# The gates of the second token group in another order on VectorE and ScalarE, and one last store in one piece

## The chip, the cores and the metric

The kernel runs on one core of one Trainium2 chip. The metric is the device time of one execution in microseconds; the number that is compared is the median over runs. Engines are named as in the profile: PE is TensorE (matmuls), PEld its weight loads, DVE is VectorE, ACT is ScalarE, POOL is GpSimd and SP is SyncE, which only issues DMAs here.

## What is computed

Three layers follow each other: an attention with global and local keys (2 x 8 heads, 768 positions, 64 wide), a first MoE block with a softmax and a layer norm, and a second block, `moe2`. The change lies in the second block alone:

```python
def _moe2_ref(x, w_in, w_out):          # x 1536 x 512, w_in 512 x 2048, w_out 2048 x 512
    h = x @ w_in
    g = h * (1.0 / (1.0 + np.exp(-h)))
    return (g @ w_out).astype(np.float32)
```

The gate is computed as (tanh(h / 2) + 1) * h, and the factor 0.5 is put on the output.

## The kernel before

The 1536 tokens are two groups of 768. Every float32 operand of a matmul is kept as two parts, a high one (`gh`, a copy in the matmul's reduced format, made by ScalarE) and a low one (`gl`, the difference, made by VectorE), and each product is three matmuls: high x high, high x low and low x high. Attention, the first block and the first group's second block are put in order by a list written out by hand (`ORDER`) and by loops behind it. All instructions of one engine run in the order in which the program text issues them.

The second group's up projection `h = x @ w_in` is done in `seven(i, fill, hook)`, L744, for eight steps `i`, each with 256 columns of `w_in`. A step forms its four blocks of h (two halves of the columns, two halves `s` of the tokens) from seven products P1 to P7, of six matmuls each, instead of eight. On TensorE a step runs

- P1 and P6 (`two`, L748), then a fill,
- P2 and P7, a fill,
- P5 and P4, a fill,
- P3, a fill.

A fill is `down` (L603): nine matmuls of the down projection with one gated block of the step before, so that TensorE has work while VectorE and ScalarE empty the products. In step 0 the fills are the last six matmuls of each of group 1's three output blocks, and `done` (L617) then copies that block out and stores it; for the third block this is an ACTIVATE of 128x1024 at L641 and a store issued on ScalarE's queue, from the buffer `sraw`.

PSUM has four tiles: three hold the output of `down`, so there is one for the products, and the next pair of products waits until the last one has been read. P1 is copied by ScalarE (L756) into `a`; VectorE adds up the rest (L746): `u = p6 + a`, then `a = p2 + a` and `b = p7 + u`, then `c = p5 + b`, `u = p5 + u`, `b = b - p4`, then `u = p3 + u`. The four tiles a, c, b, u are then the four blocks of h, and each goes through `gate` (L735): tanh on ScalarE into a buffer `e2` (two of them, L738), the gate on VectorE (L739), the high copy on ScalarE (L740); the low part (L733) is put on the list `later` and made by VectorE at the next call of `lows()`. Before the change the order in a step is: lows, gate a after P2 and P7, lows and gate c after P5 and P4, lows and gate b after P3, the last fill, gate u.

`hook` holds the weight sums for the next step (steps 1 to 6; in step 0 the splits of inputs `xprep`, in step 7 nothing): `wraw` (L694, VectorE, writes `sraw`) behind P1 and P6, `wsum` behind P2 and P7 (four adds of VectorE, L701 to L704, and the high copy L705 of 128x1024 on ScalarE), `wlow` (L709, VectorE) behind P3. P3, P5, P6 and P7 use these sums.

At the end `done` stores the three output blocks of group 2, 512 KB each: block 0 is copied by ScalarE (L641), block 1 by VectorE (L639), block 2 in halves, one by ScalarE (L633) and one by VectorE (L630), with a store for each half (L634 on ScalarE's queue, L631 on SP's).

Of the kernel before, what the change touches and what calls it, by code (L numbers as in the profile page):

```python
# [8 lines left out]
F32 = mybir.dt.float32  # L9
# [4 lines left out]
ACTF = mybir.ActivationFunctionType  # L14
ALU = mybir.AluOpType
# [41 lines left out]
def kernel(ctx, tc, q, k, v, n_global, n_local, w_in, w_out, g_ln, w2_in, w2_out, out):  # L57
    nc = tc.nc
    B, H, S, D = 2, 8, 768, 64
    NT, DM = out.shape  # L60
# [31 lines left out]
    ea = ExitStack()  # L92
# [12 lines left out]
    def f(ap):  # L105
        return ap.bitcast(F32)

    def psum():
        return ps.tile([128, 2, 512], F32, tag="p", name="p")
# [400 lines left out]
    for half in range(2):  # L510
        for kk in range(KD):
            c = slice(half * 512, half * 512 + 512)
            unit(wiw[kk * 128:(kk + 1) * 128, c, :], 0, lambda kk=kk, c=c: (wih[:, kk, c], wil[:, kk, c]))
    for half in range(2):
        for kk in range(0, KF, 2):
            c = slice(half * 256, half * 256 + 256)
            src = wow[kk * 128:(kk + 2) * 128, c, :].rearrange("(k p) n t -> p k n t", p=128)
# [16 lines left out]
    for i in range(NP):  # L534
        for j in range(2):
            c = slice(2 * j, 2 * j + 2)
            src = w2iw[j * 256:(j + 1) * 256, i * 256:(i + 1) * 256, :].rearrange("(k p) n t -> p k n t", p=128)
# [49 lines left out]
    def up(g, m, nbg=0):  # L587
        up_mm(g, m)
        up_act(g, m)
        up_mul(g, m)  # L590
        for s in range(2):
            e, hi, lo = gs[g, m, s]
            hilo(e, hi, lo)
            gs[g, m, s] = hi, lo
        bg(nbg)
# [3 lines left out]
    def words4(dt):  # L599
        x = cv.tile([128, 512, 2], I32, tag="cx", name="cx", bufs=CX)  # L600
        return x.rearrange("p n t -> p (n t)").bitcast(dt)
# [15 lines left out]
    def done(g, t3):  # L617
        o = acc[g][t3]
        rows = out.rearrange("(g s t p) d -> g t p s d", g=NG, s=2, p=128)[g, t3]
        if g == 0 and t3 == 1:  # L620
            for h in range(2):
                y = x2b[h][h].rearrange("p k n -> p (k n)")[:, 0:DM]
                nc.scalar.activation(out=y, in_=o[:, h], func=ACTF.Copy, scale=0.5)
                nc.sync.dma_start(out=rows[:, h], in_=y)
            return
        if g == 1 and t3 == 2:
            for h in range(2):
                y = words4(F32)[:, 0:DM]
                if h:
                    nc.vector.tensor_scalar(out=y, in0=o[:, h], scalar1=0.5, scalar2=None, op0=ALU.mult)  # L630
                    nc.sync.dma_start(out=rows[:, h], in_=y)  # L631
                else:
                    nc.scalar.activation(out=y, in_=o[:, h], func=ACTF.Copy, scale=0.5)  # L633
                    nc.scalar.dma_start(out=rows[:, h], in_=y)  # L634
            return
        y = sraw if g == 0 else words4(F32)
        y = y.rearrange("p (s n) -> p s n", s=2)
        if g and t3 == 1:
            nc.vector.tensor_scalar(out=y, in0=o, scalar1=0.5, scalar2=None, op0=ALU.mult)  # L639
        else:  # L640
            nc.scalar.activation(out=y, in_=o, func=ACTF.Copy, scale=0.5)  # L641
        (nc.sync if t3 == 1 else nc.scalar).dma_start(out=rows, in_=y)
# [74 lines left out]
    def product(i, n, p):  # L717
        src, k0, c, r = PROD[n]
        wh, wl = (w2h[i], w2l[i]) if src == "A" else sw[i]
        xh, xl = xop[r]  # L720
        c = slice(c * 128, (c + 1) * 128)
        j = 0
        for x, w in ((xh, wh), (xl, wh), (xh, wl)):
            for k in range(2):
                nc.tensor.matmul(p[:, 0:HG], lhsT=w[:, k0 + k, c], rhs=x[:, k, :], start=(j == 0), stop=(j == 5))  # L725
                j += 1

    later = []

    def lows():  # L730
        while later:
            e, hi, lo = later.pop(0)
            nc.vector.tensor_tensor(out=lo, in0=e, in1=f(hi), op=ALU.subtract)  # L733

    def gate(m, s, src):  # L735
        e = wk.tile([128, HG], F32, tag="e2", name="e2", bufs=2)
        hi, lo = (wk.tile([128, HG], F32R, tag=x, name=x, bufs=4) for x in ("gh", "gl"))
        nc.scalar.activation(out=e, in_=src, func=ACTF.Tanh, scale=0.5)  # L738
        nc.vector.scalar_tensor_tensor(out=e, in0=e, scalar=1.0, in1=src, op0=ALU.add, op1=ALU.mult)  # L739
        nc.scalar.activation(out=hi, in_=e, func=ACTF.Copy)  # L740
        later.append((e, hi, lo))
        gs[1, m, s] = hi, lo

    def seven(i, fill, hook):  # L744
        def add(dst, x, y, op=ALU.add):
            nc.vector.tensor_tensor(out=dst, in0=x, in1=y, op=op)  # L746

        def two(x, y):  # L748
            p = psum()
            for n, o in ((x, p[:, 0]), (y, p[:, 1])):  # L750
                product(i, n, o)
            return p[:, 0, 0:HG], p[:, 1, 0:HG]

        a, u, b, c = (cv.tile([128, 512], F32, tag="cc", name="cc", bufs=4)[:, 0:HG] for _ in range(4))
        p1, p6 = two("P1", "P6")
        nc.scalar.activation(out=a, in_=p1, func=ACTF.Copy)  # L756
        add(u, p6, a)
        lows()
        hook[0]()
        fill[0]()  # L760
        p2, p7 = two("P2", "P7")
        add(a, p2, a)
        add(b, p7, u)
        hook[1]()
        gate(2 * i, 0, a)
        fill[1]()
        p5, p4 = two("P5", "P4")
        add(c, p5, b)
        add(u, p5, u)
        add(b, b, p4, ALU.subtract)  # L770
        lows()
        gate(2 * i + 1, 1, c)
        fill[2]()
        p3 = psum()[:, 0]
        product(i, "P3", p3)
        add(u, p3[:, 0:HG], u)
        lows()
        hook[2]()
        gate(2 * i + 1, 0, b)
        fill[3]()  # L780
        gate(2 * i, 1, u)

    def guard():
        V = nc.vector
# [53 lines left out]
    with tc.manual_schedule():  # L838
        masks()
        for x in toks:  # L840
            nm, t = x.split(":")
            if nm == "CA":
                ea1.close()
                w2a = eb.enter_context(tc.tile_pool(name="w2a", bufs=1, side="right"))
                for i in range(2):
                    w2alloc(w2a, i)
            elif nm == "WK":
                ea.close()
                wk = eb.enter_context(tc.tile_pool(name="wk", bufs=1, side="right"))
                x2h = wk.tile([128, KD, G], F32R, name="x2h")  # L850
                x2l = wk.tile([128, KD, G], F32R, name="x2l")
            else:
                OPS[nm](int(t))
        fast = nc.values_load(flag, min_val=0, max_val=1)
        e1.close()
        w2b = eb.enter_context(tc.tile_pool(name="w2b", bufs=1, side="left"))
        for i in range(2, NP):
            w2alloc(w2b, i)
        bg(2)

        def fills(i):
            return [lambda z=z: down(1, *z) for z in ((2 * i, 0), (2 * i + 1, 1), (2 * i + 1, 0), (2 * i, 1))]

        def none():
            pass

        for z in range(2):
            down(0, 0, z)
        for m in range(2, KF2):
            if m < KF2 - 1:  # L870
                up(0, m, 2)
            else:
                up_mm(0, m)
                xprep(4)
                up_act(0, m)
                up_mul(0, m)
                xprep(9)
                up_hi(0, m)
                up_lo(0, m)
                xprep(5)  # L880
            for z in range(2):
                down(0, m - 1, z)
            if 10 <= m < 14:
                xprep(m - 10)
            if m == 13:
                sraw = words4(F32)
                sparts = [[words4(F32R) for _ in range(2)] for _ in range(2)]
            if 13 <= m < 15:
                wraw(m - 13)
                wsum(m - 13)  # L890
                wlow(m - 13)
        fill = [lambda t3=t3: [down(0, KF2 - 1, z, [t3]) for z in range(2)] for t3 in range(3)] + [none]
        for i in range(NP):
            if i == 0:
                hook = [lambda: [xprep(n) for n in (6, 7)], lambda: xprep(8), none]
            elif i < NP - 1:
                hook = [lambda: wraw(i + 1), lambda: wsum(i + 1), lambda: wlow(i + 1)]
            else:
                hook = [none] * 3
            seven(i, fill, hook)  # L900
            fill = fills(i)
        lows()
        for z in fill:
            z()
    eb.close()
# [2 lines left out]
    with tc.If(fast == 0):  # L908
# [12 lines left out]
        with tc.tile_pool(name="ga", bufs=1, side="left") as ga:  # L921
# [17 lines left out]
            with tc.For_i(0, B, 1) as bi, tc.For_i(0, H, 1) as hi:  # L939
                t3 = ga.tile([128, TB, D], F32, name="gv")  # L940
# [9 lines left out]
                for qb in range(TB):  # L950
# [31 lines left out]
                    o = psum()[:, 0, 0:D]  # L982
# [6 lines left out]
        with tc.tile_pool(name="gm", bufs=1, side="left") as gm:  # L989
# [8 lines left out]
            for src, dst, kk, c in full:  # L998
                units.append((src[kk * 128:(kk + 1) * 128, c * 512:(c + 1) * 512, :], 0, None, None))
                i = len(units) - 1  # L1000
# [7 lines left out]
            with tc.For_i(0, NTILE, 1) as ti:  # L1008
# [9 lines left out]
                e = gm.tile([128, FF], F32, name="ge")  # L1018
                u = gm.tile([128, FF], F32, name="gu")
# [78 lines left out]
```

## Time and profile before

| what | us |
|---|---|
| median of 3 runs (508.32 to 509.53) | 508.57 |
| the profiled execution, its own time | 509.89 |
| its span, from the first to the last instruction | 508.1 |
| TensorE busy in the span | 481.9 |
| VectorE busy | 378.3 |
| ScalarE busy | 268.4 |

The profile is of one execution, and all durations below are its. The busy share of an engine is an average over stages with different limits; the stage of the change is the last quarter of the span, from 365 us on, and it is read from the timeline: when each instruction started, how long it took, and what ended the idle time ahead of it. A matmul's start is to be relied on more than its end, which is modelled.

### The profile page before, as it was taken

The page shows a single profiled execution, that of the slowest core. Times are in us where ns is not written, and L with a number is a line of the kernel's source. Part 1 is how long each engine was busy: PE and PEld are TensorE (multiplying, and loading weights), DVE is VectorE, ACT ScalarE, POOL GpSimd, SP SyncE. Part 2 cuts the span into 40 slices and gives each one's busy share as a digit, 9 for nine tenths or more (in the row PEclk, how much of TensorE's full clock was granted, in tenths as well). Part 3 has the DMA queues.
Part 4 walks back from the last instruction along what each step waited for, and adds up shares of the span by engine and source line. Part 5 has one row for each costly group of instructions (what it writes and reads, how often), then busy time and mean ns, then how long its engine had stood idle before and what let it go on. Part 6 is the DMA issues. An engine that isn't in the chain of part 4 may idle for free.

```text
span 508.1 us, 8172 instructions
## 1 busy us (share of the span) xinstructions
PE 481.9 (95%) x2980; PEld 425.3 (84%) x2980; DVE 378.3 (74%) x847; ACT 268.4 (53%) x595; POOL 113.1 (22%) x149
## 2 busy tenths in 40 slices
PE   2789999999999999999999999999998999999993
PEld 2467789889888898999999999998887988889882
DVE  6999899866486577763698989998866676767651
ACT  5888997775566656443354545543562234232331
POOL 3664631221212233410233333332000000000000
PEclk9899999999999999999999999999998999999998
DMA  7964452332023021200324343300030000000003
GB/s 230 308 174 139 125 160 91 104 106 84 1 84 105 9 75 38 89 2 0 125 84 131 119 148 102 124 2 0 1 124 0 2 0 1 0 1 0 2 1 130
DMA packets 26115, 38.35 MB, mean 75 GB/s; under 512 B 1484, under 2 KB 13780, under 8 KB 26068
## 3 DMA queue, kind: packets, MB, share of 16 engines
q1 hardware_dynamic: 24580, 35.66, 21.9%
q10 hardware_dynamic: 1488, 2.10, 1.1%
q8 instruction: 25, 0.41, 0.3%
q14 instruction: 22, 0.18, 0.1%
HBM read 34.61 MB, written 3.15 MB: 74 GB/s over the span
## 4 chain that ended last, share of the span: by engine, by line
PE 89%; DVE 4%; DMA 2%; ACT 2%; issue 1%; SPq 1%; ACTq 0%; DVEq 0%
PE p L612 25%; PE p L499 14%; PE p L559 13%; PE p L415 12%; PE p L725 11%; PE p L357 4%; PE p L376 4%; PE p L310 3%; PE p L479 2%; DMA g<-in_moe_g_ln_dram 2%; DVE cc L147 1%; DVE A L329 1%; DMA cx<-in_moe_w_out_dram 1%; DVE cc L145 0%; ACT cx L641 0%
## 5 line engine op out<-in xcount | busy, mean ns | idle before, releaser
L612 PE MATMUL p<-w3h,gl 128*128 128x512 f32 x192 | 75.6, 394 | 0.0
L612 PE MATMUL p<-w3l,gh 128*128 128x512 f32 x192 | 75.5, 393 | 0.0
L612 PE MATMUL p<-w3h,gh 128*128 128x512 f32 x192 | 75.1, 391 | 0.0
L149 DVE SCALAR_TENSOR_TENSOR cc<-cx,cc 128x512 uint32<-128x512 uint32 x48 | 58.6, 1224 | 0.1
L415 PE MATMUL p<-wih,xT 128*128 128x512 f32 x192 | 50.5, 405 | 0.9 <-DVE negmax L329 0.9
L335 ACT ACTIVATE A<-A,negmax 128x256 f32<-128x256 f32 (+1 forms) x96 | 46.0, 481 | 8.6 <-DVE negmax L329 7.9
L329 DVE CUSTOM_DVE_ANT_0 A<-p,bias 128x256 f32<-128x256 f32 (+1 forms) x96 | 35.1, 395 | 15.4 <-PE p L357 10.3
L612 PEld LDWEIGHTS p<-w3h,gl 128*128 128x128 f32 x192 | 36.1, 188 | 7.8
L612 PEld LDWEIGHTS p<-w3l,gh 128*128 128x128 f32 x192 | 36.2, 188 | 6.4
L612 PEld LDWEIGHTS p<-w3h,gh 128*128 128x128 f32 x192 | 36.2, 189 | 6.2
L415 PEld LDWEIGHTS p<-wih,xT 128*128 128x128 f32 x192 | 34.4, 189 | 8.3 <-DVE negmax L329 1.1
L746 DVE TENSOR_TENSOR cc<-p,cc 128x384 f32<-128x384 f32 x48 | 25.2, 553 | 20.7 <-PE p L725 11.9
L170 POOL TENSOR_TENSOR w3l<-cc,w3h 128x512 fp32r<-128x512 f32 x16 | 23.4, 1462 | 60.4 <-ACT w3h L130 49.2
L740 ACT ACTIVATE gh<-e 128x384 fp32r<-128x384 f32 x32 | 16.8, 526 | 37.0 <-DVE e L739 36.4
L147 DVE SCALAR_TENSOR_TENSOR cc<-cx,cc 128x512 uint32<-128x512 uint32 x48 | 35.3, 738 | 0.1
L132 POOL TENSOR_SCALAR A<-A,sm 128x256 f32<-128x256 f32 (+1 forms) x34 | 20.3, 606 | 63.2 <-DVE sm L340 41.8
L705 ACT ACTIVATE cx<-cx 128x1024 fp32r<-128x1024 f32 x8 | 8.5, 1061 | 45.1 <-DVE cx L704 45.1
L739 DVE SCALAR_TENSOR_TENSOR e<-e,cc 128x384 f32<-128x384 f32 x32 | 17.7, 554 | 19.2 <-ACT e L738 19.2
L574 DVE SCALAR_TENSOR_TENSOR e<-e,p 128x384 f32<-128x384 f32 x32 | 16.3, 549 | 20.9 <-ACT e L568 20.9
L310 PE MATMUL p<-rk,rq 64*128 64x256 f32 (+1 forms) x192 | 26.9, 418 | 2.3 <-DMA rq<-in_q_dram 1.4
L568 ACT ACTIVATE e<-p 128x384 f32<-128x384 f32 x32 | 13.9, 487 | 27.3 <-PE p L559 27.3
L559 PE MATMUL p<-x2h,w2h 128*128 128x384 f32 x128 | 27.7, 338 | 0.0
(166 smaller groups left out, 1109.7 us busy)
## 6 DMA issues: line engine op xcount, KB each, us to landing
cx<-in_moe_w_in_dram SPq DMA_DIRECT2D x24, 512.0 KB, 3.7
cx<-in_moe_w_out_dram SPq DMA_DIRECT2D x24, 512.0 KB, 3.4
rq<-in_q_dram SPq DMA_DIRECT2D x12, 256.0 KB, 6.3
vf<-in_v_dram SPq DMA_DIRECT2D x12, 256.0 KB, 4.4
rk<-in_k_dram SPq DMA_DIRECT2D x11, 256.0 KB, 4.2
out_dram<-cx ACTq DMA_DIRECT2D x3, 512.0 KB, 3.3
out_dram<-x2b SPq DMA_DIRECT2D x2, 256.0 KB
out_dram<-cx SPq DMA_DIRECT2D x1, 512.0 KB, 4.2
```

The source lines that it names most:

```text
L147: V.scalar_tensor_tensor(out=y, in0=x[:, :, 0].bitcast(U32), scalar=29, in1=y, op0=ALU.logical_shift_right, op1=ALU.bitwise_or)
L149: V.scalar_tensor_tensor(out=y, in0=x[:, :, 1].bitcast(U32), scalar=0x80000000, in1=y, op0=ALU.bitwise_and, op1=ALU.bitwise_or)
L170: eng.tensor_tensor(out=lo, in0=w, in1=f(hi), op=ALU.subtract)
L310: nc.tensor.matmul(p[:, a, j, 0:128 * len(ks)], lhsT=rq[z, t % 3, pr, :], rhs=rk[z, W, pr, :], start=True, stop=True)
L329: nc.vector.tensor_tensor_reduce(out=x[:, c, 0:n], in0=p[:, a, j, 0:n], in1=bb, scale=-0.125, scalar=1e30, op0=ALU.add, op1=ALU.min, accum ...
L335: nc.scalar.activation(out=x[:, c, 0:n], in_=x[:, c, 0:n], func=ACTF.Exp, bias=negmax[:, t * H + h:t * H + h + 1], scale=-1.0, accum_out=s ...
L415: nc.tensor.matmul(p[:, half, :], lhsT=x[:, a, kk, :], rhs=w[:, kk, n], start=(i == 0), stop=(i == 11))
L499: nc.tensor.matmul(p[:, d], lhsT=x[:, kk, c], rhs=y[:, kk, sl], start=(i == 0), stop=(i == 3 * KF - 1))
L559: nc.tensor.matmul(p, lhsT=w[m // 2][:, kk, c], rhs=x[:, kk, s * HG:(s + 1) * HG], start=(i == 0), stop=(i == 11))
L612: nc.tensor.matmul(o, lhsT=x[:, c], rhs=w[m // 2][:, m % 2, :], start=(n == 0 and i == 0), stop=(n == KF2 - 1 and i == 2))
L725: nc.tensor.matmul(p[:, 0:HG], lhsT=w[:, k0 + k, c], rhs=x[:, k, :], start=(j == 0), stop=(j == 5))
L746: nc.vector.tensor_tensor(out=dst, in0=x, in1=y, op=op)
```

## The change

Group 2's gate is taken apart into `tanh`, `gated`, `high` and `low`, which issue one instruction each. In a step the order becomes: after P1 and P6 the copy of P1 and the add for P6, then high u of the step before (`rest`), low b of the step before, the hook, low u of the step before; after P2 and P7 the two adds, tanh a, the hook, gate a, high a; after P5 and P4 the three adds, tanh c, low a, gate c, tanh b, high c; the third fill; after P3 its add, gate b, low c, tanh u, high b, the hook, gate u. The instructions are the same as before. Behind the last step the high copy and the two lows that are left are issued. Block 2 of group 2 has no branch of its own in `done` any more: it is copied whole by ScalarE (L641) and stored by one store on ScalarE's queue.

```diff
--- before.py
+++ after.py
@@ -623,16 +623,6 @@
                 nc.scalar.activation(out=y, in_=o[:, h], func=ACTF.Copy, scale=0.5)
                 nc.sync.dma_start(out=rows[:, h], in_=y)
             return
-        if g == 1 and t3 == 2:
-            for h in range(2):
-                y = words4(F32)[:, 0:DM]
-                if h:
-                    nc.vector.tensor_scalar(out=y, in0=o[:, h], scalar1=0.5, scalar2=None, op0=ALU.mult)
-                    nc.sync.dma_start(out=rows[:, h], in_=y)
-                else:
-                    nc.scalar.activation(out=y, in_=o[:, h], func=ACTF.Copy, scale=0.5)
-                    nc.scalar.dma_start(out=rows[:, h], in_=y)
-            return
         y = sraw if g == 0 else words4(F32)
         y = y.rearrange("p (s n) -> p s n", s=2)
         if g and t3 == 1:
@@ -727,19 +717,25 @@
 
     later = []
 
-    def lows():
-        while later:
-            e, hi, lo = later.pop(0)
-            nc.vector.tensor_tensor(out=lo, in0=e, in1=f(hi), op=ALU.subtract)
-
-    def gate(m, s, src):
+    def low():
+        e, hi, lo = later.pop(0)
+        nc.vector.tensor_tensor(out=lo, in0=e, in1=f(hi), op=ALU.subtract)
+
+    def tanh(src):
         e = wk.tile([128, HG], F32, tag="e2", name="e2", bufs=2)
+        nc.scalar.activation(out=e, in_=src, func=ACTF.Tanh, scale=0.5)
+        return e
+
+    def gated(e, src):
+        nc.vector.scalar_tensor_tensor(out=e, in0=e, scalar=1.0, in1=src, op0=ALU.add, op1=ALU.mult)
+
+    def high(m, s, e):
         hi, lo = (wk.tile([128, HG], F32R, tag=x, name=x, bufs=4) for x in ("gh", "gl"))
-        nc.scalar.activation(out=e, in_=src, func=ACTF.Tanh, scale=0.5)
-        nc.vector.scalar_tensor_tensor(out=e, in0=e, scalar=1.0, in1=src, op0=ALU.add, op1=ALU.mult)
         nc.scalar.activation(out=hi, in_=e, func=ACTF.Copy)
         later.append((e, hi, lo))
         gs[1, m, s] = hi, lo
+
+    rest = []
 
     def seven(i, fill, hook):
         def add(dst, x, y, op=ALU.add):
@@ -755,30 +751,42 @@
         p1, p6 = two("P1", "P6")
         nc.scalar.activation(out=a, in_=p1, func=ACTF.Copy)
         add(u, p6, a)
-        lows()
+        if rest:
+            high(*rest.pop())
+            low()
         hook[0]()
+        if i:
+            low()
         fill[0]()
         p2, p7 = two("P2", "P7")
         add(a, p2, a)
         add(b, p7, u)
+        ea = tanh(a)
         hook[1]()
-        gate(2 * i, 0, a)
+        gated(ea, a)
+        high(2 * i, 0, ea)
         fill[1]()
         p5, p4 = two("P5", "P4")
         add(c, p5, b)
         add(u, p5, u)
         add(b, b, p4, ALU.subtract)
-        lows()
-        gate(2 * i + 1, 1, c)
+        ec = tanh(c)
+        low()
+        gated(ec, c)
+        eb_ = tanh(b)
+        high(2 * i + 1, 1, ec)
         fill[2]()
         p3 = psum()[:, 0]
         product(i, "P3", p3)
         add(u, p3[:, 0:HG], u)
-        lows()
+        gated(eb_, b)
+        low()
+        eu = tanh(u)
+        high(2 * i + 1, 0, eb_)
         hook[2]()
-        gate(2 * i + 1, 0, b)
+        gated(eu, u)
+        rest.append((2 * i, 1, eu))
         fill[3]()
-        gate(2 * i, 1, u)
 
     def guard():
         V = nc.vector
@@ -899,7 +907,9 @@
                 hook = [none] * 3
             seven(i, fill, hook)
             fill = fills(i)
-        lows()
+        high(*rest.pop())
+        low()
+        low()
         for z in fill:
             z()
     eb.close()
```

## Rows read from the trace of the kernel before

**Rows 1.** Page, part 1: busy us (share of span) x instructions

```profile
PE 481.9 (95%) x2980; PEld 425.3 (84%) x2980; DVE 378.3 (74%) x847; ACT 268.4 (53%) x595; POOL 113.1 (22%) x149
```

**Rows 2.** Timeline, PE, steps 1, 2, 7: start us, us, engine, line, operation, tiles

```profile
376.63 0.87 PE L725 MATMUL p<-x2a,w2h 128*128 128x384 f32 x4
...
396.26 0.86 PE L725 MATMUL p<-x2a,w2h 128*128 128x384 f32 x4
...
476.12 0.86 PE L725 MATMUL p<-x2a,w2h 128*128 128x384 f32 x4
...
489.71 0.39 PE L612 MATMUL p<-w3h,gh 128*128 128x512 f32 x1
```

**Rows 3.** Chain that ended last: start us, us, what; a fill in step 6

```profile
474.20 2.08 PE p L612 x9
```

**Rows 4.** Windows: us, PE, PEld, DVE, ACT, POOL busy; PEclk, DMA share, GB/s

```profile
381.00:381.50 0.50, 0.00 (x0) 0.00 (x0) 0.48 (x1) 0.00 (x0) 0.00 (x0) 1.00 0.00 0
...
384.00:384.50 0.50, 0.50 (x3) 0.50 (x2) 0.50 (x1) 0.00 (x0) 0.00 (x0) 0.50 0.00 0
```

**Rows 5.** Timeline, end of step 0 to P2 of step 1

```profile
377.32 1.01 ACT L641 ACTIVATE cx<-p 128x1024 f32<-128x1024 f32 x1
378.37 0.38 ACTq L642 DMA_DIRECT2D out_dram<-cx  x1
378.79 0.53 ACT L738 ACTIVATE e<-cc 128x384 f32<-128x384 f32 x1 [0.46 <-ACT cx L641]
...
379.95 0.53 ACT L740 ACTIVATE gh<-e 128x384 fp32r<-128x384 f32 x1 [0.63 <-DVE e L739]
380.38 0.51 ACT L738 ACTIVATE e<-cc 128x384 f32<-128x384 f32 x1
380.58 0.40 PE L612 MATMUL p<-w3h,gl 128*128 128x512 f32 x1
...
381.94 0.47 ACT L756 ACTIVATE cc<-p 128x384 f32<-128x384 f32 x1
382.45 0.56 DVE L746 TENSOR_TENSOR cc<-p,cc 128x384 f32<-128x384 f32 x1 [0.97 <-ACT cc L756]
383.06 1.08 PE L725 MATMUL p<-x2h,w2h 128*128 128x384 f32 x4 [2.08 <-DVE cc L746]
```

**Rows 6.** Timeline of step 2

```profile
397.31 1.20 PE L725 MATMUL p<-x2h,cx 128*128 128x384 f32 x6
...
405.48 1.06 ACT L705 ACTIVATE cx<-cx 128x1024 fp32r<-128x1024 f32 x1 [5.85 <-DVE cx L704]
...
406.98 0.56 DVE L739 SCALAR_TENSOR_TENSOR e<-e,cc 128x384 f32<-128x384 f32 x1 [1.54 <-ACT e L738]
407.46 1.01 DVE L746 TENSOR_TENSOR cc<-p,cc 128x384 f32<-128x384 f32 x2
408.39 0.55 DVE L746 TENSOR_TENSOR cc<-cc,p 128x384 f32<-128x384 f32 x1
408.99 1.31 PE L725 MATMUL p<-x2a,cx 128*128 128x384 f32 x6
...
411.28 1.22 DVE L709 TENSOR_TENSOR cx<-cx 128x1024 fp32r<-128x1024 f32 x1
```

**Rows 7.** Timeline of step 7: the adds for P5, then P3

```profile
486.78 1.02 DVE L746 TENSOR_TENSOR cc<-p,cc 128x384 f32<-128x384 f32 x2 [2.44 <-PE p L725]
...
488.66 1.21 PE L725 MATMUL p<-x2a,cx 128*128 128x384 f32 x6
```

**Rows 8.** Timeline, the last output block

```profile
500.33 0.60 ACT L633 ACTIVATE cx<-p 128x512 f32<-128x512 f32 x1 [0.51 <-PEq L908]
500.96 0.69 DVE L630 TENSOR_SCALAR cx<-p 128x512 f32<-128x512 f32 x1 [0.27 <-ACT cx L633]
501.68 0.40 SPq L631 DMA_DIRECT2D out_dram<-cx  x1
```

**Rows 9.** Windows at the end, columns as in rows 4

```profile
504.00:504.50 0.50, 0.00 (x0) 0.00 (x0) 0.00 (x0) 0.00 (x0) 0.00 (x0) 0.50 1.04 397
```

## The prediction, made before the changed kernel was run

> **What bounds the kernel now.** I read the page's busy table first: TensorE is busy for 95% of the span [rows 1], so only an order that lets TensorE run with fewer pauses or at a faster clock can pay. The change lies in the last stage, the eight steps of `seven`, so I went on to TensorE's timeline there. The reader should compare the starts of P1, the first product of a step. Step 1 begins at 376.63 and step 2 at 396.26, which is 19.63 us; from step 2 to step 7 there are five steps in 79.86 us, 15.97 each [rows 2]. Step 7, the last, has no weight sums to do beside its matmuls. From its P1 to the first matmul of its last fill it takes 13.59 us [rows 2], and a fill of nine matmuls takes 2.08 [rows 3]. So a step without a pause is 15.67 us. Against that, step 1 loses 3.96 us and steps 2 to 6 lose 0.30 each, 1.50 together: 5.46 us are there to be had in this stage, and no more.
>
> Where they go: in step 1 TensorE's last fill matmul starts at 380.58 and P2 only at 383.06, released by VectorE's L746 [rows 5]. The fill's pitch is 2.08 / 9 = 0.23, so P2 could have started at 380.81: a wait of 2.25 us. Behind it the granted clock is 0.50, the 1.2 GHz level, where it was 1.00 during the wait [rows 4]; the slow matmuls make up the rest of the 3.96, 1.71 us. In steps 2 to 6 the pause is ahead of P3: it starts 408.99 - 396.26 = 12.73 us into step 2, and 488.66 - 476.12 = 12.54 into step 7 [rows 2, 6, 7]; the other 0.1 is P3's own slow start (1.31 for six matmuls against 1.21).
>
> **The change part by part.** *Step 1's wait.* There is one PSUM tile for the products, so P2 waits until VectorE's `u = p6 + a` has read P6, and that waits for ScalarE's copy of P1 (L756). ScalarE runs its queue in order. Before, the queue between the large output copy L641 of group 1 and L756 holds tanh b, high b, tanh u, high u, and between these it waits twice for VectorE's L739: 378.79 to 381.94 [rows 5]. Afterwards tanh b stands ahead of L641, and high u (the `rest`) behind the copy. What is left between is tanh u and high b. Neither should wait there: high c ends ahead of L641 (377.32), and the low c that frees tanh u's buffer follows on VectorE behind at most one gate and one low of 0.56 us each (an L739 of [rows 6] for both), so by 378.6; high b's input is done in the same stretch. So, from rows 5: tanh u 378.79 (still behind the store's issue on ScalarE's queue at 378.37), high b one pitch later (380.38 - 379.95 = 0.43), the copy another 0.43 later at 379.65, the add 382.45 - 381.94 = 0.51 later, P2 383.06 - 382.45 = 0.61 later: 380.77. TensorE is ready at 380.81. The wait is gone with 0.04 us to spare, and with it the slow clock. Gain 3.96, or 3.7 if some tenths remain; I take 3.9.
>
> L641 itself must not move: it stood behind high c before and does so still. Tanh b, new ahead of high c, has to wait for the low of gate a (two `e` buffers); VectorE does that low just ahead of gate c, whose end high c needs anyway, so it has a pitch of 0.47 (407.46 - 406.98, [rows 6]) on VectorE to run in and costs 0 to 0.1.
>
> *Steps 2 to 6.* Before, tanh a stands behind the 1.06 us copy of the weight sums L705, so gate a (L739) starts at 406.98 and the first add that empties P5 only at 407.46, 11.20 us into the step [rows 6]. In step 7 without L705 the add starts at 10.66 [rows 7]. Afterwards tanh a is ahead of the sums, gate a runs right behind the sums' last add, which L705 waited for and which had ended at 405.46 (405.48 less a handover of 0.02), and is over at 406.0; VectorE is free when P4 ends, as in step 7. The third add ends about 0.5 us earlier, ahead of P3. Gain 5 x 0.30 = 1.50; between 0 (another wait is next) and 1.50 I take 1.5, since step 7's rows are the same matmuls in the same order. High a still stands behind L705: it is needed only by the next step's first fill.
>
> *What is moved on VectorE.* No gate instruction is added or removed. The wait of VectorE that is new is at the start of step 1: the weight sum L694 writes the buffer that group 1's last store (378.37) reads, and the adds for P2 and P7 are now close behind it. It is asked for near 381.1; by 381.00 no DMA moves a byte [rows 4], so it waits 0 to 0.5 us, and the adds are wanted only when P7 ends, two microseconds later. Cost nothing. The other is the low weight half L709: gate b now stands ahead of it (+0.47), but it is wanted by the last two matmuls of the next step's P6. P6 starts 397.31 - 396.26 = 1.05 into a step, four matmuls of 1.05 / 6 later they start, at 1.75. L709 started at 15.02 into step 2 and took 1.22; afterwards 15.2 to 16.4, against 15.67 + 1.75 = 17.42. One microsecond of cover.
>
> SP's queue loses one store and POOL has no work in this stage.
>
> *The last store.* Group 2's third output block is no longer copied in halves. Before: ScalarE's half at 500.33, VectorE's at 500.96, that is, behind the end of the first (its idle time is put down to L633), the last store issued at 501.68 [rows 8]. Afterwards one copy of 128x1024, 1.01 us (L641, [rows 5]) from 500.33, so its issue stands near 501.4. That is 0.3 us earlier, but the same 1.5 MB are then on their way, and the DMA share is 1.04 at 504 [rows 9]: the transfer decides and not the issue. From -0.3 to +0.6 (one 512 KB store at the end of one queue instead of two halves on two); I take -0.1.
>
> The Trainium skill says otherwise on the halves: "PSUM — Partial Sum Buffer", section "Specifications (TRN2)", has ScalarE and VectorE read PSUM side by side at full bandwidth as long as the banks differ (the halves are 512 floats each, one bank by the same page). The row disagrees: VectorE's half begins when ScalarE's is over. By the page alone the halves, begun together at 500.33, would be done by 501.02, the whole copy would be 0.3 later, and the sum would end 0.4 us higher.
>
> **The sum.** 3.9 + 1.5 + 0.1 = 5.5 us, all on TensorE's path save the last tenth. The profiled execution has a span of 508.1 and a time of 509.89, 1.79 around the span; it would become 502.6 and 504.4. The median of the three runs is 508.57, 1.32 below the profiled run; the same 5.5, less 0.1 for what step 1 may keep, takes it to 503.2.
>
> **The rivals.** (A) The pause ahead of P3 stays: VectorE is late for P5 for another reason, the four sums themselves. For it: VectorE has the longest list in that stretch. Against it: L705 started at 405.48, a microsecond before gate a. Then 503.2 + 1.5 = 504.7. (B) A part of step 1's wait stays, as its margin is only 0.04: if tanh u or the store's issue on ScalarE comes a microsecond late, TensorE waits one and may fall to the slow clock as it did behind 381.0: 503.2 + 1.0 + 1.7 = 505.9. (C) The single last store ends later, +0.6 to +0.9: about 504.0. (D) Slower than before: L709 is late in each of steps 1 to 6, since it now stands behind gate b and low c, which hang on tanh b and high c. Place: the last two matmuls of P6. It decides from 1.0 us later than worked out above; each further microsecond costs six, so 2.2 us late gives 6 x 1.2 = 7.2 us: 503.2 + 7.2 = 510.4. Against it: ScalarE is idle 5.85 us ahead of L705 [rows 6], so its queue isn't full. (E) The order doesn't do what it says: the wait is for group 1's output copy, which still stands ahead of the copy of P1, and TensorE's gain is given back at the next fill: about 508. Against it: the work between the two is half as long.
>
> **How the numbers follow.** Forecast 503.2, chance 0.61; its own range is 502.4 to 504.0 (the last store 0.3 either way, a few tenths of step 1 and the scatter of the runs). A 0.12, B 0.10, C 0.08, E 0.05, D 0.04. The range takes in A, C and most of B: 502.3 to 505.6. 0.3% of the time is 1.5 us, about what a measurement of this kernel can tell from no change. The forecast and A, B and C lie below 507.0: faster 0.91. E is the same, 0.05, and D slower, 0.04.
>
> **What would show it right or wrong.** Right: P1 of step 1 to P1 of step 2 takes 15.7 to 15.9 us, at a granted clock of 1.00; the later steps 15.7; gate a starts ahead of P4's end; ScalarE has two instructions between L641 of group 1 and the copy of P1. Wrong: a wait of TensorE for VectorE ahead of P2 in step 1 or ahead of P3 in the others; a wait for the low weights in P6; or a last store that lands more than 5 us behind the last matmul.

## The result and the profile after

The changed kernel takes 504.57 us (502.56 to 505.46) where the kernel before, run beside it, takes 508.51 (507.20 to 509.75). The ratio is 0.9915 with an interval of 0.9889 to 0.994, so it is faster by 4.3 us (3.1 to 5.6). The profiled execution took 504.35 us with a span of 502.6; before it was 509.89 and 508.1.

In the changed code the lines have moved: the products are L715, the copy of P1 is L752, the adds behind the products L742, tanh L726, the gate's product L730, the high copy L734, the low part L722. The weight sums are L684 to L694, their copy L695, the low weight half L699, the output copies L629 and L631, the stores L632.

TensorE's line of the busy table [rows 1] is now:

```profile
PE 478.8 (95%) x2980; PEld 424.5 (84%) x2980; DVE 376.2 (75%) x846; ACT 269.9 (54%) x595; POOL 113.2 (23%) x149
```

The share is the same 95%, with 3.1 us less of busy time. So this table alone doesn't tell what was gained: part of it is pauses, part is matmuls that ran at the slow clock. The starts of P1 tell it, as in [rows 2]. TensorE's timeline of the changed kernel, steps 1, 2 and 7, and the first matmul of the last fill:

```profile
376.34 0.87 PE L715 MATMUL p<-x2a,w2h 128*128 128x384 f32 x4
...
392.06 0.86 PE L715 MATMUL p<-x2a,w2h 128*128 128x384 f32 x4
...
470.53 0.86 PE L715 MATMUL p<-x2a,w2h 128*128 128x384 f32 x4
...
484.14 0.39 PE L612 MATMUL p<-w3h,gh 128*128 128x512 f32 x1
```

Step 1 takes 392.06 - 376.34 = 15.72 us (19.63 before), the five steps behind it 78.47, 15.69 each (15.97 before), and step 7's stretch to the fill 13.61 (13.59 before). Read the same way, this is where the 5.5 us of the two spans went; "stage" is from the first P1 to the start of the last matmul, "tail" from there to the span's end:

| | P1 of step 0 at | step 1 | step 2 | steps 3 to 6, each | stage | tail | span |
|---|---|---|---|---|---|---|---|
| before | 364.94 | 19.63 | 15.96 | 15.96 to 15.99 | 134.79 | 8.37 | 508.1 |
| after | 364.63 | 15.72 | 15.70 | 15.69 to 15.70 | 129.53 | 8.44 | 502.6 |

5.26 us are gained in the stage, 0.31 ahead of it, where nothing was changed, and the tail is 0.07 longer.

The timeline of the changed kernel around the start of step 1, beside [rows 5]:

```profile
377.03 1.01 ACT L631 ACTIVATE cx<-p 128x1024 f32<-128x1024 f32 x1
...
378.49 0.53 ACT L726 ACTIVATE e<-cc 128x384 f32<-128x384 f32 x1 [0.45 <-ACT cx L631]
...
378.92 0.51 ACT L734 ACTIVATE gh<-e 128x384 fp32r<-128x384 f32 x1
...
379.34 0.47 ACT L752 ACTIVATE cc<-p 128x384 f32<-128x384 f32 x1
...
379.84 0.56 DVE L742 TENSOR_TENSOR cc<-p,cc 128x384 f32<-128x384 f32 x1 [0.23 <-ACT cc L752]
...
380.29 0.40 PE L612 MATMUL p<-w3h,gl 128*128 128x512 f32 x1
...
380.45 0.65 PEld L715 LDWEIGHTS p<-x2h,w2h 128*128 128x128 f32 x4 [0.20 <-DVE cc L742]
380.53 0.89 PE L715 MATMUL p<-x2h,w2h 128*128 128x384 f32 x4
...
380.84 1.23 DVE L684 TENSOR_TENSOR cx<-w2h,w2l 128x1024 f32<-128x1024 f32 x1
```

Between the output copy L631 and the copy of P1 stand one tanh and one high copy, neither with a wait for VectorE. The copy of P1 starts at 379.34 (381.94 before), and P2 follows the fill's last matmul without an idle time in its row; before it had 2.08 there. Its weight load (PEld) did wait 0.20 for VectorE's add, so nothing is left to spare. At 384 us the granted clock is 1.00, the 2.4 GHz level, where [rows 4] show 0.50:

```profile
384.00:384.50 0.50, 0.50 (x4) 0.38 (x3) 0.47 (x2) 0.02 (x1) 0.00 (x0) 1.00 0.00 0
```

Step 2 of the changed kernel, beside [rows 6]:

```profile
391.59 1.22 DVE L699 TENSOR_TENSOR cx<-cx 128x1024 fp32r<-128x1024 f32 x1
...
399.19 0.53 ACT L726 ACTIVATE e<-cc 128x384 f32<-128x384 f32 x1 [3.93 <-DVE cc L742]
...
400.84 0.42 DVE L694 TENSOR_TENSOR cx<-cx 128x256 f32<-128x256 f32 x1
...
401.19 0.55 DVE L730 SCALAR_TENSOR_TENSOR e<-e,cc 128x384 f32<-128x384 f32 x1
401.30 1.06 ACT L695 ACTIVATE cx<-cx 128x1024 fp32r<-128x1024 f32 x1 [1.59 <-DVE cx L694]
...
402.74 1.02 DVE L742 TENSOR_TENSOR cc<-p,cc 128x384 f32<-128x384 f32 x2 [1.01 <-PE p L715]
...
404.63 1.21 PE L715 MATMUL p<-x2a,cx 128*128 128x384 f32 x6
```

Tanh a now stands ahead of the sums' copy L695, gate a (L730) runs right behind the last sum, and the adds that empty P5 start when P4's matmuls release them and not when VectorE comes free: 402.74 - 392.06 = 10.68 us into the step, against 11.20 before and 10.66 in step 7 [rows 6, 7]. P3 starts at 12.57 (12.73 before) and takes 1.21 instead of 1.31.

The last output block, beside [rows 8], and the window near the end, beside [rows 9]:

```profile
494.28 0.38 ACTq L632 DMA_DIRECT2D out_dram<-cx  x1
...
494.76 1.02 ACT L631 ACTIVATE cx<-p 128x1024 f32<-128x1024 f32 x1 [0.51 <-PEq L918]
495.16 0.38 SPq L632 DMA_DIRECT2D out_dram<-cx  x1
495.82 0.69 ACTq L632 DMA_DIRECT2D out_dram<-cx  x1
```

```profile
498.50:499.00 0.50, 0.00 (x0) 0.00 (x0) 0.00 (x0) 0.00 (x0) 0.00 (x0) 1.00 1.00 365
```

The three stores of 512 KB start their issue within 1.6 us of each other, and the DMA engines are then full (share 1.00).

### The profile page after: what moved, and what is told of

Its sections match the earlier page's. It is cut to its first block, busy times and chain, and to the rows that moved or that the text cites. A ratio compares the mean times of both kernels' runs of the same rounds, so it can differ in the third digit from the quotient of the medians.

```text
span 502.6 us, 8155 instructions
## 1 busy us (share of the span) xinstructions
PE 478.8 (95%) x2980; PEld 424.5 (84%) x2980; DVE 376.2 (75%) x846; ACT 269.9 (54%) x595; POOL 113.2 (23%) x149
## 4 chain that ended last, share of the span: by engine, by line
PE 88%; DVE 3%; ACT 3%; DMA 3%; SPq 1%; issue 1%; POOL 0%; ACTq 0%; DVEq 0%
PE p L612 26%; PE p L499 14%; PE p L559 13%; PE p L715 12%; PE p L415 11%; PE p L357 4%; PE p L376 3%; PE p L310 3%; PE p L479 2%; DMA cx<-in_moe_w_in_dram 2%; DVE cc L147 1%; DVE A L329 1%; DMA cx<-in_moe_w_out_dram 1%; ACT A L335 1%; ACT woh L130 1%
## 5 line engine op out<-in xcount | busy, mean ns | idle before, releaser
L742 DVE TENSOR_TENSOR cc<-p,cc 128x384 f32<-128x384 f32 x48 | 25.3, 554 | 32.2 <-PE p L715 21.7
L726 ACT ACTIVATE e<-cc 128x384 f32<-128x384 f32 x32 | 16.8, 526 | 52.1 <-DVE cc L742 34.4
L499 PE MATMUL p<-lnh,woh 128*128 128x256 f32 x192 | 27.7, 287 | 0.0
L559 PE MATMUL p<-x2l,w2h 128*128 128x384 f32 x128 | 27.5, 335 | 0.0
```

The costliest lines, as they stand in the source:

```text
L499: nc.tensor.matmul(p[:, d], lhsT=x[:, kk, c], rhs=y[:, kk, sl], start=(i == 0), stop=(i == 3 * KF - 1))
L559: nc.tensor.matmul(p, lhsT=w[m // 2][:, kk, c], rhs=x[:, kk, s * HG:(s + 1) * HG], start=(i == 0), stop=(i == 11))
```

## The experiments

The theory is that two things which don't touch each other are gained: the order ahead of the copy of P1 takes away step 1's wait, and tanh a ahead of the sums takes away the pause ahead of P3. Against it stand the rivals A to E of the prediction. Each kernel's median is compared with that of the kernel before run beside it; steps are read from the starts of P1.

**One part alone.** e1 is the kernel before with tanh a alone moved; its `gate` then leaves out its own tanh:

```diff
+        ea = tanh(a)
         hook[1]()
-        gate(2 * i, 0, a)
+        gate(2 * i, 0, a, ea)
```

> The kernel before with one part of the change: tanh a is issued ahead of the weight sums, so ahead of the copy L705 on ScalarE; gate a and all else stay. Theory: the pause ahead of P3 in steps 2 to 6 goes (steps of 15.67 us instead of 15.97) and step 1 keeps its wait of about 2.2 us and the slow clock behind it: stage (first P1 to the start of the last matmul) 134.8 - 1.5 = 133.3 us, time 1.5 us below before. Rival A (the four sums are the cause, not L705): steps stay at 15.97, time as before.

e2 is the changed kernel with tanh a behind the sums, as it was, and the last store in halves, as it was:

```diff
-        ea = tanh(a)
         hook[1]()
+        ea = tanh(a)
```

> The change without the early tanh a (it stands behind the weight sums and L705 again) and with the last block stored in halves as before. Theory: step 1 takes 15.7 to 16.0 us with the clock at 1.00, the pause ahead of P3 comes back in the steps with sums (15.97 each): stage about 131.0, time 3.9 us below before. Rival: one order needs the other, and step 1 keeps a part of its wait; then the time is 0 to 2 us below before.

e3 is the kernel before with the branch of the two halves taken out, e4 the changed kernel with that branch put back:

```diff
-        if g == 1 and t3 == 2:
-            for h in range(2):
-                ...
-            return
```

> The kernel before with the last output block copied whole by ScalarE and stored by one store. Theory: the 1.5 MB on their way decide, so from the start of the last matmul to the span's end it stays at 8.4 us within 0.3. Rival C: 0.6 to 0.9 longer. Rival (the issue decides): 0.3 shorter.

> The change with the last block stored in halves as before. Theory: stage as in the changed kernel, 129.5 us, and the tail 8.4 us within 0.3; time equal to the changed kernel's. Rival C: 0.6 to 0.9 us faster than the changed kernel.

Measured, all four beside the same runs of the kernel before (510.03 us); the rows "before" and "after" are the traces of the section above:

| | step 1 | later steps | stage | tail | median | ratio |
|---|---|---|---|---|---|---|
| before | 19.63 | 15.96 to 15.99 | 134.79 | 8.37 | 510.03 | |
| e1, tanh a alone | 18.01 | 15.70, step 6 15.92 | 132.09 | 8.41 | 508.08 | 0.996 (0.9944 to 0.9976) |
| e2, all but tanh a and the store | 16.03 | 15.98 to 16.00 | 131.32 | 8.36 | 506.18 | 0.9927 (0.9904 to 0.9951) |
| e3, store alone | 18.33 | 15.99 | 133.58 | 7.80 | 509.05 | 0.9984 (0.9969 to 0.9999) |
| e4, all but the store | 15.73 | 15.69 | 129.53 | 8.33 | 504.92 | 0.9894 (0.9875 to 0.9913) |
| after | 15.72 | 15.69 to 15.70 | 129.53 | 8.44 | | |

Tanh a is worth 0.3 us in each step and nothing of step 1's wait; the order of the gates is worth step 1's wait and nothing in the later steps. The gains in the medians are 1.95 for e1, 3.85 for e2 and 5.11 for e4, which holds both: they add up within their intervals. The timeline of e1 in step 2:

```profile
404.26 0.55 DVE L743 SCALAR_TENSOR_TENSOR e<-e,cc 128x384 f32<-128x384 f32 x1
404.38 1.06 ACT L705 ACTIVATE cx<-cx 128x1024 fp32r<-128x1024 f32 x1 [1.59 <-DVE cx L704]
...
405.82 1.02 DVE L750 TENSOR_TENSOR cc<-p,cc 128x384 f32<-128x384 f32 x2 [1.01 <-PE p L725]
...
407.70 1.21 PE L725 MATMUL p<-x2a,cx 128*128 128x384 f32 x6
```

and that of e2:

```profile
402.87 1.06 ACT L705 ACTIVATE cx<-cx 128x1024 fp32r<-128x1024 f32 x1 [6.05 <-DVE cx L704]
...
404.37 0.56 DVE L740 SCALAR_TENSOR_TENSOR e<-e,cc 128x384 f32<-128x384 f32 x1 [1.54 <-ACT e L736]
404.85 1.02 DVE L752 TENSOR_TENSOR cc<-p,cc 128x384 f32<-128x384 f32 x2
...
406.38 1.32 PE L725 MATMUL p<-x2a,cx 128*128 128x384 f32 x6
```

In e1 the gate stands ahead of the copy L705 and the adds wait for TensorE (1.01); in e2 the gate waits 1.54 for its tanh, the adds follow it, and P3 takes 1.32. That is the pause, and rival A falls. The 0.22 more of e1's step 6 is made at P2, whose weight load waits 0.39 for the add: the copy of P1 ahead of it stands behind a high copy that waits 0.96 for its gate, where it waits 0.69 in step 5.

The last store can't be read from these: the tail is 8.37 and 8.33 with halves, 8.44 and 7.80 whole, and the ratios point opposite ways (e3, whole, is about 0.8 us below the kernel before; e4, with halves, has a lower ratio than the changed kernel's 0.9915). But e3 showed something else. Its step 1 is 18.33 us and not 19.63, with the same wait as before:

```profile
382.12 0.96 PE L715 MATMUL p<-x2h,w2h 128*128 128x384 f32 x4 [2.07 <-DVE cc L736]
```

```profile
384.00:384.50 0.50, 0.50 (x4) 0.50 (x3) 0.14 (x1) 0.00 (x0) 0.00 (x0) 1.00 0.00 0
```

The first fence is its timeline, the second its window at 384: the granted clock stayed at 1.00. It stayed in e1 too, whose P2 has an idle time of 2.06; that is why its stage is 132.09 where 133.3 was expected. e10 is the kernel before, unchanged:

> The kernel before once more, for its granted clock behind the wait in step 1. If the clock falls behind that wait in each execution: step 1 takes 19.6 us as in the profile of before. If in some: 18.0 to 18.4 in the others, as in the runs with tanh a alone and with the whole store alone, which kept this wait and a clock of 1.00.

It took 509.56 us (509.54 the kernel before beside it), its step 1 19.62, its stage 134.82, its tail 8.94. P2's row in its timeline, and the window:

```profile
382.15 1.09 PE L725 MATMUL p<-x2h,w2h 128*128 128x384 f32 x4 [2.06 <-DVE cc L746]
```

```profile
384.00:384.50 0.50, 0.50 (x3) 0.50 (x3) 0.16 (x1) 0.00 (x0) 0.00 (x0) 0.50 0.00 0
```

The clock fell to 0.50. Four traces hold a wait of 2.06 to 2.08 us at this place: in two the clock fell behind it, in two it did not, and the step differs by 19.63 - 18.33 = 1.30 us. What tells the two apart is left open. The traces do differ in one thing long before: near 22 us the granted clock stood at 0.50 for about 3.5 us in the two where it later fell, and for about 7 us in the two where it stayed. That this decides is not shown. The tail of one and the same kernel was 8.37 in one trace and 8.94 in another, so a store worth some tenths can't be seen in single traces.

**Is the copy of P1 the cause?** e5 keeps the changed order but puts high u back at the end of its own step, so that it stands on ScalarE ahead of the copy of P1 again:

```diff
-        if rest:
-            high(*rest.pop())
+        if i:
             low()
...
-        rest.append((2 * i, 1, eu))
         fill[3]()
+        high(2 * i, 1, eu)
```

> The change with high u issued in its own step again, so ahead of the copy of P1 in ScalarE's queue; the low of u stays where it was. Theory (the queue between the output copy and the copy of P1 sets P2's start in step 1): high u waits for gate u, the copy comes 0.7 us later (379.34 to about 380.1), P2 of step 1 waits 0.6 to 0.8 us, step 1 takes 16.3 to 16.5 us, the others 15.7: 0.7 us slower than the change. Rival E (the output copy itself is what is waited for): step 1 stays at 15.7.

e6 leaves the order as changed and adds, in step 1 alone, copies of a 128x128 tile onto itself ahead of the copy of P1, four or ten; this is added work:

```diff
+        if i == 1:
+            for _ in range(4):
+                nc.scalar.activation(out=ident, in_=ident, func=ACTF.Copy)
         nc.scalar.activation(out=a, in_=p1, func=ACTF.Copy)
```

> The change with four copies of a 128x128 tile onto itself on ScalarE ahead of the copy of P1 in step 1 (added work, the output is the same). By the 128x128 ACTIVATEs' 0.39 us, less what overlaps, they take 1.2 to 1.5 us. Theory: P2 of step 1 waits 1.1 to 1.4 us; whether the granted clock falls behind such a wait is open: at 1.00 step 1 takes 16.8 to 17.2, at 0.50 up to 1.7 more.

> As with four copies, with ten: 3.0 to 3.8 us. Theory: P2 of step 1 waits 3.0 to 3.7 us, longer than the kernel before waited there, and the granted clock falls to 0.50 behind it: step 1 takes 18.7 to 21.2 us. Rival (the clock in the profile of before fell for another reason than the wait): the clock stays at 1.00 and step 1 takes 18.7 to 19.4.

e5 took 505.51 us, ratio 0.9927 (0.9898 to 0.9956), step 1 16.49, later steps 15.70. Its timeline:

```profile
380.54 0.53 ACT L734 ACTIVATE gh<-e 128x384 fp32r<-128x384 f32 x1 [0.21 <-DVE e L730]
380.97 0.47 ACT L752 ACTIVATE cc<-p 128x384 f32<-128x384 f32 x1
...
382.09 0.98 PE L715 MATMUL p<-x2h,w2h 128*128 128x384 f32 x4 [0.50 <-DVE cc L742]
```

High u waits for its gate, the copy waits behind it, and P2 waits 0.50; the step is 0.77 longer. The wait in the row counts from the end of the fill's last matmul, which is 0.40 long at a pitch of 0.23, so 0.17 more is lost, and P2 itself takes 0.09 more than in the changed kernel. The two e6 kernels, in one run each, took 505.50 and 508.73 us. The timeline with four copies, and then with ten:

```profile
379.79 1.32 ACT L754 ACTIVATE ident<-ident 128x128 f32<-128x128 f32 x4
381.02 0.47 ACT L755 ACTIVATE cc<-p 128x384 f32<-128x384 f32 x1
...
382.13 0.97 PE L715 MATMUL p<-x2h,w2h 128*128 128x384 f32 x4 [1.00 <-DVE cc L742]
```

```profile
378.74 3.37 ACT L754 ACTIVATE ident<-ident 128x128 f32<-128x128 f32 x10
...
382.01 0.47 ACT L755 ACTIVATE cc<-p 128x384 f32<-128x384 f32 x1
...
383.13 1.65 PE L715 MATMUL p<-x2h,w2h 128*128 128x384 f32 x4 [3.04 <-DVE cc L742]
```

Four copies put the copy of P1 back by 381.02 - 379.79 = 1.23 us; step 1 is 16.97, 1.25 longer. So there is no slack left ahead of P2: what is put ahead of the copy comes out of TensorE one for one. Ten copies take 382.01 - 378.74 = 3.27; step 1 is 20.56, 4.84 longer, and the 1.57 above the 3.27 are put down to the slow clock, which the window of that kernel shows:

```profile
384.00:384.50 0.50, 0.50 (x3) 0.50 (x2) 0.50 (x1) 0.00 (x0) 0.00 (x0) 0.50 0.00 0
```

Behind the waits of 0.50 and 1.00 the clock stayed at 1.00. Rival E, that the output copy ahead sets the time, falls: that copy was in its place in all of them.

**Rival D, the low weight half.** e7 is the changed kernel with the low half L699 computed two or three times over, each time with the same result, so that it ends later; this is added work:

```diff
-                hook = [lambda: wraw(i + 1), lambda: wsum(i + 1), lambda: wlow(i + 1)]
+                hook = [lambda: wraw(i + 1), lambda: wsum(i + 1), lambda: [wlow(i + 1) for _ in range(2)]]
```

> The change with the low half of the weight sums (wlow) computed twice in a row in steps 1 to 6, the same values, one more VectorE instruction of 1.22 us (a pitch of 1.13). Theory of rival D: cover of about 1.0 us, so P6's last matmuls wait 0.1 to 0.2 us in each of steps 2 to 7: steps 15.8 to 15.9 us. If the cover is larger: 15.70.

> As with wlow twice, with three in a row (2.27 us more). Theory: P6 waits 1.2 to 1.4 us in each of steps 2 to 7, steps 16.9 to 17.1 us, 7 to 8 us slower than the change, the clock at 1.00. If the granted clock falls behind each wait: more.

In one run each they took 506.56 us with two and 515.75 with three, where the kernel before took 509.54. Step 1, whose half is formed once, keeps 15.73; from step 2 on a step takes 16.08 to 16.13 with two, on average 0.41 more than the 15.69 of the changed kernel, and 17.38 to 17.39 with three, 1.69 more. Both are longer than expected (15.8 to 15.9, and 16.9 to 17.1). The timeline with three, where step 2's P1 starts at 393.45:

```profile
392.98 3.74 DVE L699 TENSOR_TENSOR cx<-cx 128x1024 fp32r<-128x1024 f32 x3
...
394.32 0.71 PEld L715 LDWEIGHTS p<-x2h,cx 128*128 128x128 f32 x4
...
396.77 0.30 PEld L715 LDWEIGHTS p<-x2h,cx 128*128 128x128 f32 x2 [1.73 <-DVE cx L699]
396.77 0.62 PE L715 MATMUL p<-x2h,cx 128*128 128x384 f32 x2 [1.42 <-DVE cx L699]
```

The last two matmuls of P6 wait, as the prediction had it, but their weight load waits first: it could have begun at 394.32 + 0.71 = 395.03, 1.58 us into the step. The matmuls were put at 1.75, and e7's own rows give the same: the four ahead of them start at 394.49 with a pitch of about 0.17, so 395.2 (the 1.42 in the row counts from a modelled end, later than that). The half ends 0.75 us into a step in the changed kernel (391.59 + 1.22 - 392.06), so the cover is 0.83. Both runs give the same from the steps: two halves end 1.25 later and cost 0.41, three end 2.52 later and cost 1.69, which leaves 0.84 and 0.83. Behind the waits of 1.42 the clock stayed at 1.00.

**What is still to be had in the tail.** The traces after show the DMA engines full behind the last matmul, so the stores should begin earlier and not be issued faster. The fills of the last stretch finish one 512-wide half of each block before the other. e8 is the changed kernel with each half of group 2's blocks copied and stored as soon as its own matmuls are done; `half` copies `acc[1][t3][:, s]` and stores it, on VectorE and SP's queue for block 1, on ScalarE and its queue for blocks 0 and 2:

```diff
-            if left[g, t3, s] == left.get((g, t3, 1 - s)) == KF2:
+            if g and n + 1 == KF2:
+                half(t3, s)
+            elif left[g, t3, s] == left.get((g, t3, 1 - s)) == KF2:
```

> The change with each half of group 2's three output blocks copied and stored as soon as its own sum is done: the first halves one fill (2.08 us) earlier, six stores of 256 KB instead of three of 512 KB. Theory (the 1.5 MB on their way decide the end): from the start of the last matmul to the span's end 5.9 to 6.9 us instead of 8.4, time 1.5 to 2.5 us below the change. Rival: TensorE waits for the copies of the first halves, which share their PSUM tiles with the last fill, and the gain is given back: 0 to 0.5 us below the change.

It took 503.00 us (501.93 to 503.32), ratio 0.9871 (0.9842 to 0.9901), with the stage as in the changed kernel (129.55) and a tail of 7.13 instead of 8.44. The end of its timeline, and a window there:

```profile
492.02 0.35 ACTq L629 DMA_DIRECT2D out_dram<-cx  x1
...
494.80 0.60 ACT L628 ACTIVATE cx<-p 128x512 f32<-128x512 f32 x1 [0.42 <-PE p L612]
495.42 1.07 ACTq L629 DMA_DIRECT2D out_dram<-cx  x1
```

```profile
495.00:495.50 0.50, 0.00 (x0) 0.00 (x0) 0.00 (x0) 0.39 (x1) 0.00 (x0) 1.00 0.48 168
```

The first store starts 2.35 us ahead of the start of the last matmul (492.02 against 494.37), where the changed kernel's first starts 0.12 behind it (494.28 against 494.16), and the share falls to 0.48 before the last one comes: the transfer is no longer one full stretch, which speaks for the last matmul, its copy and its store as what ends last now. The tail is 1.3 us shorter, less than expected (5.9 to 6.9 us was); the medians, 503.00 and 504.57, differ by 1.6, inside the 1.5 to 2.5 expected of the time. One row stands out: the issue of the last store takes 1.07 us, three times the 0.35 of the others. e9 issues the stores of the first block on SP's queue too, so that ScalarE's queue has two stores instead of four:

```diff
-        (nc.sync if t3 == 1 else nc.scalar).dma_start(out=rows, in_=y)
+        (nc.scalar if t3 == 2 else nc.sync).dma_start(out=rows, in_=y)
```

> The change with early half stores, with block 0's two stores issued on SP's queue instead of ScalarE's, so that the last store has one ahead of it on its queue and not three. Theory (the long issue of the last store, 1.07 us against 0.35, comes from what is queued ahead of it): the last issue is 0.35 to 0.4 us long and the tail from the start of the last matmul 6.2 to 6.8 us instead of 7.13. Rival (the DMA engines as a whole decide): 7.1 as before.

It took 503.32 us, ratio 0.9882 (0.9862 to 0.9902), tail 7.32 where 6.2 to 6.8 was expected. Its timeline:

```profile
492.83 4.65 SPq L629 DMA_DIRECT2D out_dram<-cx  x4
...
496.23 0.35 ACTq L629 DMA_DIRECT2D out_dram<-cx  x1
```

ScalarE's last issue is back at 0.35 us, but one of SP's four now takes 1.84, and the tail is no shorter. That the stores queued ahead on the same queue make the issue long is not shown: in the kernels with the old halves the second store on ScalarE's queue, with one ahead of it, took 1.11 us (before), 1.09 (e1), 1.12 (e4), 0.78 (e2) and 0.60 (e10, the same kernel as before). The tail was longest, 8.94, with the shortest of these issues. e8 is the best of the kernels run; that it beats the changed kernel rests on the tail of its trace and on the medians (503.00 and 504.57, each beside its own runs of before), while the intervals of the two ratios overlap.

## Why the prediction was right, point by point

*The wait of step 1* was worked out right. P2 was put at 380.77, 4.14 us behind P1; it started 4.19 behind it (380.53 - 376.34), with no wait in its row. The chain of pitches from [rows 5] (tanh, high, copy, add, handover) is what happened, and e6 agrees that the margin was about as small as the 0.04 in the text: 1.23 us more cost 1.25.

*The slow clock behind it* is the term that was mis-sized: 1.71 us, counted as if always there. It was worked out as what is left of the 3.96. First, 0.3 of it is the pause ahead of P3, which step 1 has as the others do (e1's step 1 is 0.32 below e3's, e2's is 0.30 above e4's); the change takes that away too, so the gain of 3.9 did not suffer by it. Second, the clock itself is 1.30 us, and falls behind this wait in only two of four traces. Where it doesn't fall, the stage gains 133.58 - 129.53 = 4.05 us, from e3; where it does, 5.26. The forecast of 5.5 took the second for certain. The measured ratios lie on both sides of the middle: 4.3 us here, 5.4 in e4. That the timed runs of before were a mixture is likely from this, but it isn't shown: only a trace has the clock at that place, and the mean granted clock of a whole run (0.985 to 0.990 wherever it is recorded) doesn't tell, as it is 0.988 or 0.989 in the traces of before, e10, e1 and e3 alike.

*The pause ahead of P3*, 1.50, was right: it measured 1.39 in steps 2 to 6 of the traces, and e1 and e2 show that tanh a alone makes it.

*Nothing for VectorE's new wait* was right: L684, the first instruction of the sums, started at 380.84 without an idle time in its row. The prediction named L694 of the kernel before; it is this line now.

*The low weight half* ended about where it was put: L699 started 391.59 - 376.34 = 15.25 us into step 1, forecast 15.2. But the cover of "one microsecond" was a step that failed: it counted to the matmuls of the low half, at 1.75 us into the step, while their weights are loaded ahead of them, at 1.58 in e7. The cover is 0.83. The mechanism of rival D is real, at six times the price: e7 with three is slower than the kernel before.

*The last store*, -0.1 between -0.3 and +0.6: e4 and the changed kernel differ by 0.1 in the tail, and one kernel differs from itself by 0.57. All the traces together say more: five with the halves (before, e10, e1, e2, e4) have tails of 8.33 to 8.94, the middle one 8.37, and seven with the whole store (after, e3, e5, both e6, both e7) 7.80 to 8.52, the middle one 8.31. So -0.1 fits, and the +0.6 to +0.9 of rival C does not. The sign named for it, a last landing more than 5 us behind the last matmul, was badly chosen: before, the store issued at 501.68 landed 4.6 later, 6.5 us behind the start of the last matmul, and in the changed kernel the one issued at 495.82 landed 5.2 later, 6.9 behind it, with hardly a difference in the tail. That the transfer decides and not the issue was right as far as e8 tells, whose earlier stores made the tail shorter. On the two halves, the Trainium skill's "PSUM — Partial Sum Buffer", section "Specifications (TRN2)", has ScalarE and VectorE read PSUM side by side at full bandwidth as long as the banks differ, by which, in the prediction's estimate, the sum would have ended 0.4 us higher. The trace of e8 agrees where the two engines copy halves of different tiles: ScalarE's copy from 493.78 (0.60 us) and VectorE's from 494.12 (0.69) overlap and take as long as those that stand alone (0.60 from 491.39, 0.69 from 492.07). With the two halves of one tile VectorE's starts when ScalarE's has ended, in all five traces that have them (idle time of 0.26 or 0.27); why is not shown, and tails that scatter by 0.57 don't decide about the 0.4.

*The sum.* The profiled execution came out at the span forecast, 502.6. That is in part luck: 0.31 us of it arose ahead of the stage, where nothing was changed (the first P1 starts anywhere from 364.02 to 366.02 in the traces of all kernels run), and stands in for what the later steps and the store gave less. The median is 504.57 against 503.2, inside the range. The 1.4 that are missing are about the size of the clock's 1.30, but that this is their cause is not shown, and the runs hold a second candidate. Three of the changed kernel's six runs have a mean granted clock of 0.992 to 0.994 and a middle time of 503.38, the other three 0.988 or 0.989 and 505.21; traces of kernels with the same steps have 0.994 where the clock stood at 0.50 near 22 us for about 3.5 us (after, e4) and 0.989 or 0.990 where it did for about 7 (e8, e9). The profiled run, 0.994, is one of the first three.

*The rivals.* A fell with e1, E with e5 and e6. Of B, the wait part did not come true, and its price of 1.7 for the clock is 1.3, at times. C did not show in the tails. D has its mechanism but not its condition.

*Left open*: what decides whether the clock falls behind a wait of about 2 us; what sets the runs of the changed kernel apart by 1.8 us; and where the long issue of a late store comes from.

## What to carry to other kernels

Where an engine runs its queue in order, cost a new order by the pitches of the instructions that stand between the release and the copy that frees the buffer: that sum was right to 0.05 us here. A loss that is read as "the rest" of a slow step holds whatever else that step does, so look in a second trace whether it comes back before it is promised as gain. And the time by which an operand that TensorE loads as weights is wanted is that of its weight load, not of its matmul; here they were 0.17 us apart.

## What the runs showed of the hardware

The granted clock fell to 0.50 behind a wait of TensorE of 2.06 to 2.08 us in two traces and stayed at 1.00 in two others; it stayed behind waits of 0.50, 1.00 and 1.42, and fell behind one of 3.04. Taken by the traces' early stretch at 0.50: with the short one it fell behind waits of 2.06, 2.08 and 3.04 and stayed behind 1.00; with the long one it stayed behind all of 0.50, 1.42, 2.06 and 2.07. So the length of the wait alone does not decide. A fall cost 1.30 us behind the waits of about 2.07, and 1.57 by difference behind that of 3.04.

The issue of a 256 KB store took 0.33 to 0.42 us in most cases, but 1.07 for the fourth on ScalarE's queue (e8), 1.84 for one of four on SP's (e9) and 1.09 to 1.12 for the second on ScalarE's in three of the five traces with the old halves, while other stores were on their way.

ScalarE and VectorE copied from two different PSUM tiles at the same time in e8 without either taking longer (0.60 and 0.69 us, as alone).
